# A new order and a new choice of engines for one fused attention, MLP and expert program

## The chip, the cores and the metric

The kernel runs on one core of one Trainium2 chip. The metric is the device time of one execution in microseconds, the median of several runs. The kernel before takes 794.45 us (median of 3 runs, 793.1 to 795.2). A difference under 0.3%, some 2.4 us, is about what a measurement of this kernel can't tell from no change.

## The reference, cut to what matters

Three layers follow each other: attention with two kinds of masks, an MLP whose gate is a cosine, and a layer with 8 experts that takes each token once, by a greedy assignment with a capacity.

```python
scores = scale * np.matmul(q, k.transpose(0, 1, 3, 2))     # 4 batches, 8 heads, 576 positions, 64
attn = softmax(where(mask, scores, -1e9))                  # heads 0-3: the last 32 positions; 4-7: every 32nd
x = (attn @ v) as [2304, 512]
h = x @ w_in;  g = h * np.cos(h);  y = g @ w_out           # 512 -> 2048 -> 512
logits = y @ w_gate                                        # 8 experts
for idx in np.argsort(-logits.flatten()):                  # a token to its best expert with room, 288 each
    ...
for e in range(8):
    out[mask] = np.maximum(y[mask] @ w1[e], 0.0) @ w2[e]   # 512 -> 1024 -> 512
```

Products are made in float16 with a high and a low part: each is three matrix products (high by high, high by low, low by high).

## The kernel before, in words

**Stages.** Attention of batch 0 and 1 in float32 and of batch 2 and 3 in float16 parts (`att_pair` L622, `att_half` L709). Layer 1 of the MLP in units of 128 columns of `w_in` (`l1_unit` L873): 24 products of 128 x 288 a unit, then on ACT and DVE the cosine and its two float16 parts, which lie in `ar_a`, `ar_b` and `ar_t`. Layer 2 in tiles of 128 tokens (`l2_tile` L986), 18 tiles, written to `y_dram`. The assignment (`route` L1021) is a long chain of small DVE instructions, and the matrix products of the last 13 tiles lie beside it on PE. The experts (`experts` L1213) end the program.

**The experts.** `expert_weights` (L1195) brings the weights of one expert in 8 loads of 512 KB from `w` into two staging buffers (`wst`, in `ar_l`). A load is made into float16 parts in two halves: for each half an ACT instruction writes the high part (an ACTIVATE of 128x512 that reads `ar_l`, into `ar_l` for experts of even number and into `ar_a` for those of odd number), then a DVE instruction writes the low part. A staging buffer is free for its next load when both of its DVE instructions are done. `layer1` (L1241) makes 8 groups of 12 products of 128 x 288 on PE; each group is taken out of PSUM by a relu on ACT (an ACTIVATE `ar_w<-psum`) and a DVE instruction for the low part. `layer2` (L1263) makes 8 groups for 4 outputs, taken out by an ACTIVATE `ar_b<-psum`. `gather` (L1219) fetches the tokens of the next expert and transposes them by DMA (3 DMA_TRANSPOSE of `ar_b`), and `store` (L1283) transposes the outputs by DMA (3 DMA_TRANSPOSE of `ar_w`), copies them and writes them out. All direct loads, stores and DMA transposes are issued by SP, in one order.

**What sets the order.** The function that describes the work doesn't issue it: every instruction, or group of matrix products, is a task that `Plan.add` (L179) records with its engine, a duration by a formula, and what it reads and writes. `Plan.order` (L217) is a list scheduler that runs when the kernel is built: it follows the engines in time, takes on each free engine the ready task with the longest path to the end, and so fixes each engine's order of instructions. On the chip each engine goes through its order as it stands. Three tables steer it: `BOOST` (L53) adds a number to the path of the tasks of one label, `CHOICE` (L97) puts an optional task on another engine (`'gl'`: the low part of the cosine on DVE or POOL, `'oh'` and `'og'`: copies of the store, `'cvo'`: the conversion of a block of `w_out`, `'exp'`: the way in which the exponential gets its bias), and `LAT` (L165) is the wait between two engines. Up to the first product with a block of `w_out`, gaps on PE that the scheduler foresees are filled with products that nobody reads (`p.filler`, L507).

Of the kernel before, what the change touches and what calls it, by code (L numbers as in the profile page):

```python
# [48 lines left out]
SWITCH = 1283.0  # L49
# [4 lines left out]
    ('att', 0, 0, 1): 579, ('att', 0, 0, 2): 6896, ('att', 0, 0, 3): 656, ('att', 0, 0, 4): 23690, ('att', 0, 1, 0): 1726,  # L54
    ('att', 0, 1, 1): 2601, ('att', 0, 1, 2): 5980, ('att', 0, 1, 3): -29, ('att', 0, 1, 4): 1804, ('att', 0, 2, 0): -529,
    ('att', 0, 2, 1): 5908, ('att', 0, 2, 2): 723, ('att', 0, 2, 3): 25775, ('att', 0, 2, 4): -70, ('att', 0, 3, 0): 1022,
    ('att', 0, 3, 1): 2929, ('att', 0, 3, 2): 209, ('att', 0, 3, 3): 20612, ('att', 0, 3, 4): 6402, ('att', 1, 0, 0): 1630,
    ('att', 1, 0, 1): 4760, ('att', 1, 0, 2): 4942, ('att', 1, 0, 3): 452, ('att', 1, 1, 0): 1309, ('att', 1, 1, 1): -15332,
    ('att', 1, 1, 3): -14442, ('att', 1, 1, 4): 7781, ('att', 1, 2, 0): -16993, ('att', 1, 2, 1): -7431, ('att', 1, 2, 2): -161,
    ('att', 1, 2, 3): -1353, ('att', 1, 2, 4): 964, ('att', 1, 3, 0): -28626, ('att', 1, 3, 1): 278, ('att', 1, 3, 2): 7133,  # L60
    ('att', 1, 3, 3): 1662, ('att', 1, 3, 4): -8348, ('att', 2, 0, 0): -6066, ('att', 2, 0, 1): -2444, ('att', 2, 0, 2): -7600,
    ('att', 2, 0, 3): 2071, ('att', 2, 1, 0): 596, ('att', 2, 1, 1): 2386, ('att', 2, 1, 2): -693, ('att', 2, 1, 3): -642,
    ('att', 2, 1, 4): -4, ('att', 2, 2, 0): -405, ('att', 2, 2, 1): 1129, ('att', 2, 2, 2): 2285, ('att', 2, 2, 3): 500,
    ('att', 2, 2, 4): 1102, ('att', 2, 3, 0): 12272, ('att', 2, 3, 1): 243, ('att', 2, 3, 2): 23127, ('att', 2, 3, 3): -4806,
    ('att', 2, 3, 4): 56132, ('att', 3, 0, 0): 3915, ('att', 3, 0, 1): 1009, ('att', 3, 0, 2): -6033, ('att', 3, 0, 3): 3149,
    ('att', 3, 0, 4): -31510, ('att', 3, 1, 1): -1244, ('att', 3, 1, 2): -1327, ('att', 3, 1, 3): 2204, ('att', 3, 1, 4): -3113,
    ('att', 3, 2, 0): 6530, ('att', 3, 2, 1): 3150, ('att', 3, 2, 3): 7677, ('att', 3, 2, 4): 21602, ('att', 3, 3, 0): 40114,
    ('att', 3, 3, 1): 25986, ('att', 3, 3, 2): 17764, ('att', 3, 3, 3): 815, ('att', 3, 3, 4): 28249, ('l1', 0, 0): 195,
# [26 lines left out]
}  # L95

CHOICE = {  # L97
# [1419 lines left out]
```

## Time and profile before

| | |
|---|---|
| median of 3 runs | 794.45 us (793.1 to 795.2) |
| the profiled execution | 796.68 us |
| its span, first to last instruction | 794.3 us |
| PE busy | 717.5 us (90%) |
| DVE, ACT, POOL busy | 527.4, 409.7, 275.7 us |
| mean granted TensorE clock | 0.974 |
| DMA | 104.14 MB, mean 131 GB/s |

The profiled execution is one run, 2.2 us above the median of the others; its span leaves out 2.4 us around the instructions. An engine's busy time is the time in which an instruction of its own runs; what an engine waited for is told in the list of waits, and windows give the busy time of each engine in a stretch of the span.

### The profile page before, as it was taken

How to read it: one execution, taken by the hardware profiler on the slowest of the kernel's cores; microseconds unless marked ns; L12 is line 12 of the kernel's file. 1: busy time of each engine (PE TensorE's matmuls, PEld its weight loads, DVE VectorE, ACT ScalarE, POOL GpSimd, SP SyncE). 2: the span in 40 equal slices, each digit the busy share in tenths (PEclk: the TensorE clock that was granted, in tenths of full speed). 3: DMA queues.
4: the chain of work that ended last, by engine and by line, in shares of the span. 5: the costliest groups of instructions: out<-in, count | busy, mean ns of one | idle time of the engine just before them, and what ended most of it. 6: DMA issues, size and time to landing. Idle time of an engine off the chain costs nothing.

```text
span 794.3 us, 18699 instructions
## 1 busy us (share of the span) xinstructions
PE 717.5 (90%) x7520; PEld 497.4 (63%) x7520; DVE 527.4 (66%) x1356; ACT 409.7 (52%) x907; POOL 275.7 (35%) x292
## 2 busy tenths in 40 slices
PE   7878888988998998999999999999898988789896
PEld 6666666764543676777654554335786766567686
DVE  4799999995767788756487777578346455644620
ACT  3556877875643689888440111024135554654532
POOL 2667476666531145335100000001521343231231
PEclk8999999999999999999899999999899999999998
DMA  8954254555767742000252000016588999989731
GB/s 241 286 167 130 72 146 114 146 130 121 165 136 194 162 96 54 20 1 1 67 162 78 28 28 14 15 43 195 139 171 209 256 246 220 241 232 238 167 71 41
DMA packets 114262, 104.14 MB, mean 131 GB/s; under 512 B 79872, under 2 KB 89856, under 8 KB 114176
## 3 DMA queue, kind: packets, MB, share of 16 engines
q1 hardware_dynamic: 111104, 93.52, 46.1%
q0 software_dynamic: 3072, 9.44, 3.8%
q8 instruction: 59, 0.97, 0.5%
q14 instruction: 27, 0.22, 0.1%
HBM read 74.36 MB, written 9.70 MB: 106 GB/s over the span
## 4 chain that ended last, share of the span: by engine, by line
PE 33%; DMA 26%; DVE 22%; ACT 12%; issue 4%; POOL 2%; SPq 1%; POOLq 0%; ACTq 0%; DVEq 0%
PE psum L358 32%; DMA ar_l<-w 14%; DVE ar_l L392 9%; DVE ar_t L392 7%; ACT ar_l L382 5%; DVE ar_a L392 3%; ACT ar_a L382 2%; ACT ar_t L382 2%; DMA ar_t<-w_in 2%; DVE ar_w L392 2%; DMA ar_b<-ar_b 1%; DMA ar_l<-ar_t 1%; DMA ar_b<-y_dram,idy 1%; DVE mxs L392 1%; DMA ar_t<-w_out 1%
## 5 line engine op out<-in xcount | busy, mean ns | idle before, releaser
L358 PEld LDWEIGHTS <-ar_l 128*128 128x128 f16 x2576 | 232.8, 99 | 99.0 <-issue 34.5
L358 PE MATMUL psum<-ar_l 128*128 128x288 f16 (+2 forms) x1578 | 205.9, 287 | 23.2 <-DVE ar_l L392 22.9
L358 PEld LDWEIGHTS <-ar_a 128*128 128x128 f16 (+1 forms) x1600 | 128.7, 99 | 94.9 <-issue 41.8
L358 PE MATMUL psum<-ar_w,ar_a 128*128 128x512 f16 (+3 forms) x1056 | 175.0, 310 | 5.6 <-DVE ar_w L392 2.3
L382 ACT ACTIVATE ar_l<-psum 128x288 int32<-128x288 f32 (+5 forms) x201 | 78.2, 412 | 92.5 <-PE psum L358 79.4
L392 DVE SCALAR_TENSOR_TENSOR ar_l<-ar_l,psum 128x288 f32<-128x288 int32 (+2 forms) x236 | 98.2, 441 | 36.1 <-ACT ar_l L382 34.8
L358 PEld LDWEIGHTS <-ar_t 128*128 128x128 f16 (+4 forms) x1980 | 74.6, 101 | 42.3 <-issue 19.0
L382 ACT ACTIVATE ar_a<-ar_l 128x512 f16<-128x512 f32 (+2 forms) x125 | 63.6, 537 | 54.6 <-DMA ar_l<-w 50.6
L392 DVE SCALAR_TENSOR_TENSOR ar_l<-ar_l 128x512 f16<-128x512 f32 (+3 forms) x94 | 52.2, 574 | 37.7 <-ACT ar_l L382 36.7
L382 ACT ACTIVATE ar_l<-ar_l,quarter 128x288 f32<-128x288 f32 x128 | 66.2, 530 | 12.6 <-DVE ar_l L392 12.0
L392 DVE SCALAR_TENSOR_TENSOR ar_t<-ar_t 128x512 uint32<-128x512 uint32 (+6 forms) x60 | 62.8, 1049 | 13.0 <-ACT ar_t L382 12.9
L392 DVE SCALAR_TENSOR_TENSOR ar_a<-ar_l,ar_a 128x512 f16<-128x512 f32 x64 | 43.5, 711 | 37.0 <-ACT ar_a L382 36.9
L437 POOL TENSOR_TENSOR ar_l<-ar_l 128x288 f32<-128x288 f32 (+1 forms) x41 | 28.0, 685 | 111.0 <-DVE ar_l L392 80.9
L382 ACT ACTIVATE ar_l<-ar_l 128x512 f16<-128x512 f32 x64 | 37.0, 621 | 55.4 <-DMA ar_l<-w 55.4
L358 PE MATMUL psum<-ar_w,ar_t 128*128 128x512 f16 (+2 forms) x288 | 63.8, 349 | 0.0
L382 ACT ACTIVATE ar_t<-ar_t 128x512 uint32<-128x512 uint32 (+12 forms) x63 | 46.2, 754 | 33.5 <-DVE ar_t L392 9.7
L358 PE MATMUL psum<-ar_w,ar_b 128*128 128x512 f16 (+1 forms) x240 | 62.6, 393 | 0.0
L358 PE MATMUL psum<-ar_b,ar_a 128*128 128x288 f16 (+3 forms) x504 | 55.2, 277 | 8.1 <-DVE ar_w L392 4.2
L358 PE MATMUL psum<-ar_b,ar_l 128*128 128x96 f16 (+1 forms) x576 | 51.2, 253 | 6.6 <-ACT ar_b L382 3.4
L1301 POOL DMA_INDIRECT out<-ar_b,idx x24 | 24.0, 999 | 84.4 <-DMA out<-ar_b,idx 18.6
L358 PE MATMUL psum<-ar_w,ar_l 128*128 128x288 f16 x384 | 47.9, 286 | 3.5 <-DVE ar_w L392 3.5
L437 POOL TENSOR_TENSOR ar_t<-ar_t 128x512 uint32<-128x512 uint32 (+7 forms) x25 | 40.5, 1623 | 20.5 <-ACT ar_t L382 19.9
(142 smaller groups left out, 881.2 us busy)
## 6 DMA issues: line engine op xcount, KB each, us to landing
ar_l<-w SPq DMA_DIRECT2D x64, 512.0 KB, 4.1
ar_t<-w_out SPq DMA_DIRECT2D x16, 512.0 KB, 3.5
ar_t<-w_in SPq DMA_DIRECT2D x12, 512.0 KB, 4.6
y_dram<-ar_l SPq DMA_DIRECT2D x13, 256.0 KB, 2.0
ar_t<-vl SPq DMA_DIRECT2D x6, 432.0 KB, 5.6
ar_t<-qs SPq DMA_DIRECT2D x4, 648.0 KB, 4.5
ar_t<-vs SPq DMA_DIRECT2D x6, 384.0 KB, 3.4
ar_t<-ql SPq DMA_DIRECT2D x4, 576.0 KB, 4.1
```

Source lines behind the costliest of these rows:

```text
L358: nc.tensor.matmul(o, l, x, start=start, stop=stop)
L382: p.add("act", ns, lambda: nc.scalar.activation(o, x, func, **kw), r, w, tab=tab)
L392: p.add("dve", 69.0 + 1.042 * n, lambda: getattr(nc.vector, name)(*args, **kw), r, w)
L437: p.add("pool", 145.0 + (rate or (1.667 if y.dtype == F32 else 1.885)) * size(o), lambda: nc.gpsimd.tensor_tensor(o, x, y, op=op), r, w)
L1301: p.add("pool", 546.0, lambda og=og, T=T: nc.gpsimd.indirect_dma_start(out[:, :], bass.IndirectOffsetOnAxis(ap=idx[:, T:T + 1], axis=0), o ...
```

## The change

`LAT` and the formulas for durations are new, and `Plan.order` is written anew. It now steps through time and follows all five engines side by side. A task on DVE and one on POOL that both carry the flag `ports` go at 0.62 and 0.77 of their rate while both run. A DMA takes SP 400 ns to issue (a transpose 152 ns for each 128 columns), and its data pass one after the other through one server with a first wait, a time by size (`work`), and at most 8 DMAs in flight. The tables `BOOST` and `CHOICE` were found anew with it. The instructions' arithmetic stays.

```diff
 BOOST = {
-    ('att', 0, 0, 1): 579, ('att', 0, 0, 2): 6896, ('att', 0, 0, 3): 656, ('att', 0, 0, 4): 23690, ('att', 0, 1, 0): 1726,
...
+    ('att', 0, 0, 0): -180, ('att', 0, 0, 1): -62086, ('att', 0, 0, 2): -8815, ('att', 0, 0, 3): -3820, ('att', 0, 0, 4): 19790,
...
 CHOICE = {
...
+    ('cvi', 0): 'pool', ('cvi', 2): 'pool', ('cvi', 9): 'pool2', ('cvi', 10): 'pool', ('cvi', 14): 'pool', ('cvo', 3): 'pool2',
...
-    LAT = {"pe": {"pe": 3.0, "act": 197.0, "dve": 196.0, "pool": 200.0, "sp": 1290.0},
-           "act": {"pe": 200.0, "act": 60.0, "dve": 142.0, "pool": 170.0, "sp": 1410.0},
...
-           "sp": {"pe": 740.0, "act": 908.0, "dve": 908.0, "pool": 908.0, "sp": 2100.0},
+    LAT = {"pe": {"pe": 3.0, "act": 197.0, "dve": 196.0, "pool": 200.0, "sp": 200.0},
+           "act": {"pe": 200.0, "act": 60.0, "dve": 142.0, "pool": 170.0, "sp": 140.0},
...
+           "sp": {"pe": 450.0, "act": 450.0, "dve": 450.0, "pool": 450.0, "sp": 300.0},
+    BESIDE = {"dve": 0.62, "pool": 0.77}
+    FIRST, FIRST_POOL, FLIGHT = 950.0, 1100.0, 8
...
-    def add(self, eng, ns, fn, r=(), w=(), tab=None, lat=None, busy=None):
+    def add(self, eng, ns, fn, r=(), w=(), tab=None, work=None, busy=None, ports=False, late=0.0):
...
     def order(self):
...
+        def rate(e):
+            i = cur[e]
+            if e == "pe":
+                look(int(now / self.WINDOW + 1e-9))
+                return 1.0 if warm[int(now / self.WINDOW + 1e-9)] else t[i][1] / self.busy[i][0]
+            if e in self.BESIDE and t[i][6]:
+                o = cur["pool" if e == "dve" else "dve"]
+                if o is not None and t[o][6]:
+                    return self.BESIDE[e]
+            return 1.0
...
+                if e == "sp":
+                    server = max(now + self.FIRST, server) + t[i][5]
+                    land[i] = server
+                    lands.append(server)
...
     def dma(o, x, nbytes, r, w):
-        p.add("sp", nbytes / 360.0, lambda: nc.sync.dma_start(o, x), r, w)
+        p.add("sp", 400.0, lambda: nc.sync.dma_start(o, x), r, w, work=nbytes / (390.0 if any(k[0] == "y" for k in w) else 240.0))
 
     def dma_t(o, x, r, w):
 
-        p.add("sp", 112.0 * x.shape[1] / 128, lambda: nc.sync.dma_start(o, x, transpose=True), r, w)
+        p.add("sp", 152.0 * x.shape[1] / 128, lambda: nc.sync.dma_start(o, x, transpose=True), r, w, work=160.0 * x.shape[1] / 128)
```

**What moves, on ACT, in layer 1 of expert 2.** `ar_w<-psum` is a relu of `layer1`, `ar_a<-ar_l` the high part of half a load of expert 3, `ar_l<-ar_l` of expert 4, and the COPY belongs to the store of expert 1. Before, from the first of these relus on:

```order
L382 ACTIVATE ar_w<-psum 128x288 x3
L382 ACTIVATE ar_a<-ar_l 128x512 x2
L382 ACTIVATE ar_w<-psum 128x288
L382 ACTIVATE ar_a<-ar_l 128x512 x2
L382 ACTIVATE ar_w<-psum 128x288
L385 COPY ar_b<-ar_w 96x512
L382 ACTIVATE ar_w<-psum 128x288
L385 COPY ar_b<-ar_w 96x512
L382 ACTIVATE ar_l<-ar_l 128x512
L382 ACTIVATE ar_w<-psum 128x288
L382 ACTIVATE ar_l<-ar_l 128x512
L382 ACTIVATE ar_w<-psum 128x288
```

And with the change, from the first relu of the same layer on:

```order
L417 ACTIVATE ar_w<-psum 128x288
L417 ACTIVATE ar_a<-ar_l 128x512 x2
L417 ACTIVATE ar_w<-psum 128x288 x3
L417 ACTIVATE ar_a<-ar_l 128x512 x2
L417 ACTIVATE ar_w<-psum 128x288
L420 COPY ar_b<-ar_w 96x512 x2
L417 ACTIVATE ar_w<-psum 128x288
L420 COPY ar_b<-ar_w 96x512
L417 ACTIVATE ar_w<-psum 128x288
L417 ACTIVATE ar_a<-ar_l 128x512 x2
L417 ACTIVATE ar_w<-psum 128x288
L420 COPY ar_b<-ar_w 96x512
```

Six halves of loads stand among the eight relus in both. Before they are the last two loads of expert 3 and the first of expert 4; now they are the fourth, fifth and sixth load of expert 3. Counted in loads, the conversions ahead of the first relu of layer 1 of the experts 1 to 7 were 22, 30, 38, 46, 53.5, 60 and 64, and are 21, 27, 33, 39, 45, 53 and 61 (8 loads belong to each expert, and layer 1 of expert e needs 8e + 4 of them).

**On ACT, layer 1 of expert 7.** Here `ar_a<-ar_l` is a half load of expert 7 itself. The rows before, from the second last load of the program on, through layer 2 of expert 6 (`ar_b<-psum`) and layer 1 of expert 7:

```order
L382 ACTIVATE ar_a<-ar_l 128x512 x2
L382 ACTIVATE ar_w<-psum 128x288
L382 ACTIVATE ar_a<-ar_l 128x512 x2
L382 ACTIVATE ar_w<-psum 128x288 x2
L382 ACTIVATE ar_b<-psum 128x288 x2
L385 COPY ar_w<-ar_b 128x3x96
L382 ACTIVATE ar_b<-psum 128x288 x2
L385 COPY ar_w<-ar_b 128x3x96 x2
L382 ACTIVATE ar_w<-psum 128x288 x6
L385 COPY ar_b<-ar_w 96x512
L382 ACTIVATE ar_w<-psum 128x288 x2
```

With the change, from the first relu of layer 1 of expert 7 on:

```order
L417 ACTIVATE ar_w<-psum 128x288 x2
L417 ACTIVATE ar_a<-ar_l 128x512 x2
L417 ACTIVATE ar_w<-psum 128x288 x2
L420 COPY ar_b<-ar_w 96x512 x2
L417 ACTIVATE ar_w<-psum 128x288
L420 COPY ar_b<-ar_w 96x512
L417 ACTIVATE ar_w<-psum 128x288
L417 ACTIVATE ar_a<-ar_l 128x512
L417 ACTIVATE ar_w<-psum 128x288
L417 ACTIVATE ar_a<-ar_l 128x512
L417 ACTIVATE ar_w<-psum 128x288
L417 ACTIVATE ar_a<-ar_l 128x512 x2
```

The last two loads were converted among the relus of expert 6, and the eight relus of expert 7 found all weights there. Now six halves, three loads, stand among the relus of expert 7, the last load behind all of them.

**On SP, the loads and transposes of the first experts.** `ar_l<-w` is a load, DMA_TRANSPOSE of `ar_w` the store of an expert, of `ar_b` the gather for the next. Before, from the third load of expert 2 on:

```order
L440 DMA ar_l<-w 128x1024 x2
L440 DMA ar_l<-w 128x2x512 x4
L444 DMA_TRANSPOSE ar_w<-ar_w 128x8x128 x3
L440 DMA ar_l<-w 128x1024 x2
L444 DMA_TRANSPOSE ar_b<-ar_b 128x8x96 x2
L440 DMA ar_l<-w 128x1024 x2
L444 DMA_TRANSPOSE ar_b<-ar_b 128x8x96
L440 DMA ar_l<-w 128x2x512 x3
L444 DMA_TRANSPOSE ar_w<-ar_w 128x8x128
L440 DMA ar_l<-w 128x2x512
L444 DMA_TRANSPOSE ar_w<-ar_w 128x8x128 x2
```

With the change, from the same load on:

```order
L478 DMA ar_l<-w 128x1024 x2
L478 DMA ar_l<-w 128x2x512 x2
L482 DMA_TRANSPOSE ar_w<-ar_w 128x8x128 x2
L478 DMA ar_l<-w 128x2x512
L482 DMA_TRANSPOSE ar_w<-ar_w 128x8x128
L478 DMA ar_l<-w 128x2x512
L478 DMA ar_l<-w 128x1024
L482 DMA_TRANSPOSE ar_b<-ar_b 128x8x96
L478 DMA ar_l<-w 128x1024
L482 DMA_TRANSPOSE ar_b<-ar_b 128x8x96 x2
L478 DMA ar_l<-w 128x1024 x2
```

The transposes of the first store stood behind six loads and stand behind four, and the third of them stands between two loads.

**Counts.** PE has 351 fillers for 185. Of the cosine's low parts of batch 0 and 1, seven go from DVE to POOL and five from POOL to DVE. The conversion of block 3 of `w_out` becomes `'pool2'`: two DVE instructions on 128x512 less, a DVE TENSOR_SCALAR, an ACT and two POOL instructions more. One pair of heads of batch 1 takes its exponentials with a bias (two DVE TENSOR_TENSOR from PSUM less, nine small ACTIVATE for two), so does one of batch 2. Batch 0 has one copy out of PSUM more on DVE and one less on ACT. ACT has 18 loads of function tables for 16. The softmax product of two pairs, and the low part of one, go from DVE to POOL in batches 2 and 3. The copies of the stores change places among ACT, DVE and POOL.

## Rows read from the trace of the kernel before

**Rows 1.** Windows: from:to, length, busy PE, PEld, DVE, ACT, POOL; clock; DMA share; GB/s.

```profile
100.00:120.00 20.00, 16.14 (x136) 12.45 (x135) 19.70 (x38) 15.61 (x40) 13.24 (x14) 1.00 0.53 139
...
200.00:220.00 20.00, 19.11 (x198) 11.65 (x196) 15.12 (x24) 15.37 (x23) 11.95 (x8) 1.00 0.75 149
...
460.00:480.00 20.00, 20.00 (x176) 10.29 (x175) 14.55 (x76) 1.92 (x3) 1.72 (x3) 1.00 0.07 27
...
640.00:660.00 20.00, 17.69 (x143) 13.71 (x141) 9.60 (x18) 9.70 (x22) 6.31 (x7) 1.00 0.90 234
```

**Rows 2.** What PE waited for, 590 to 770 us: total, times, longest.

```profile
PE psum L358 <- DVE ar_w L392: 13.3, 12, 2.2
PE psum L358 <- ACT ar_b L382: 7.1, 9, 1.5
```

**Rows 3.** What ACT waited for, 590 to 770 us.

```profile
ACT ar_l L382 <- DMA ar_l<-w: 36.8, 20, 7.5
ACT ar_a L382 <- DMA ar_l<-w: 35.9, 21, 4.1
```

**Rows 4.** Timeline of ACT, 628 to 640.5 us: start, length, instruction [idle before, releaser].

```profile
630.47 1.15 ACT L382 ACTIVATE ar_a<-ar_l 128x512 f16<-128x512 f32 x2 [2.50 <-DMA ar_l<-w]
...
634.33 1.15 ACT L382 ACTIVATE ar_a<-ar_l 128x512 f16<-128x512 f32 x2 [2.41 <-DMA ar_l<-w]
635.38 0.39 ACT L382 ACTIVATE ar_w<-psum 128x288 f16<-128x288 f32 x1
```

**Rows 5.** Timeline of PE, the same stretch.

```profile
633.35 1.63 PE L358 MATMUL psum<-ar_b,ar_l 128*128 128x288 f16 x12 [0.27 <-DVE ar_w L392]
637.21 3.47 PE L358 MATMUL psum<-ar_w,ar_l 128*128 128x288 f16 x27 [2.23 <-DVE ar_w L392]
```

**Rows 6.** Windows over the experts (columns as in rows 1).

```profile
601.90:768.50 166.60, 147.98 (x1166) 114.50 (x1165) 86.32 (x162) 87.94 (x190) 47.66 (x59) 0.99 0.86 215
...
602.00:663.80 61.80, 54.49 (x434) 42.16 (x432) 34.90 (x65) 34.78 (x76) 18.08 (x21) 1.00 0.98 242
```

**Rows 7.** Timelines of SP's DMA queue: start, length, issues.

```profile
585.95 15.41 SPq L440 DMA_DIRECT2D ar_l<-w  x6
...
706.29 1.94 SPq L440 DMA_DIRECT2D ar_l<-w  x2
...
715.82 8.24 SPq L440 DMA_DIRECT2D ar_l<-w  x4
...
744.41 1.04 SPq L440 DMA_DIRECT2D ar_l<-w  x2
```

**Rows 8.** Groups of DVE by form, 40 to 180 us: busy, mean ns | idle before.

```profile
L392 DVE SCALAR_TENSOR_TENSOR ar_t<-ar_t 128x512 uint32<-128x512 uint32 x37 | 35.5, 962 | 0.0
...
L392 DVE TENSOR_SCALAR ar_t<-ar_t 128x512 uint32<-128x512 uint32 x24 | 14.2, 591 | 0.4 <-DMA ar_t<-w_out 0.4
L392 DVE TENSOR_TENSOR ar_a<-ar_l,ar_a 128x288 f16<-128x288 f32 x13 | 8.0, 612 | 0.2
...
L392 DVE TENSOR_TENSOR ar_t<-psum,mxs 118x324 f32<-118x324 f32 x4 | 1.9, 483 | 0.0
```

**Rows 9.** Groups of POOL by form, 40 to 180 us.

```profile
L437 POOL TENSOR_TENSOR ar_a<-ar_l,ar_a 128x288 f16<-128x288 f32 x19 | 16.7, 885 | 13.4 <-ACT ar_a L382 13.4
...
L437 POOL TENSOR_TENSOR ar_t<-ar_t 128x512 uint32<-128x512 uint32 x10 | 13.6, 1356 | 6.2 <-ACT ar_t L382 6.2
```

**Rows 10.** Waits of PE, 90 to 193 us, then 193 to 385 us.

```profile
PE psum L358 <- DVE ar_l L392: 12.3, 10, 2.8
...
PE psum L358 <- DVE ar_l L392: 5.7, 5, 2.2
```

**Rows 11.** Timeline of PE, 50 to 58 us: one run of fillers and the product behind it.

```profile
52.86 3.23 PE L507 MATMUL psum<-quarter 128*128 128x128 f16 x52
56.55 0.32 PE L358 MATMUL psum<-mask,ident 128*128 128x384 bf16 x1 [0.46 <-ACT ar_t L608]
```

**Rows 12.** Groups of ACT: loads of function tables.

```profile
L382 ACT ACT_TABLE_LOAD x14 | 18.0, 1283 | 0.3
```

More of the change, by code (lines that the diff above doesn't have):

```diff
@@ L203, in add @@
         deps.discard(i)
-        self.tasks.append((eng, ns, fn, sorted(deps), tab, lat))
+        self.tasks.append((eng, ns, fn, sorted(deps), tab, work, ports, late))
         return i
@@ L215, in reuse, with wait, ways @@
         return i
-    def order(self):
+    def wait(self, i, s):
+        if self.tasks[s][0] is None:
+            return 0.0
+        return self.LAT["sp" if self.tasks[i][5] else self.tasks[i][0]][self.tasks[s][0]]
+    def ways(self):
         t = self.tasks
@@ L220, in order @@
         succ = [[] for _ in t]
-        left = [len(x[3]) for x in t]
         for i, x in enumerate(t):
@@ L240, in order @@
             path[i] = min(v for (m, _), v in top.items() if m == name) - L2_DELAY - 20.0 * k
+        return succ, path
+    def order(self):
+        t = self.tasks
+        succ, path = self.ways()
         for i, v in self.boost.items():
             path[i] += v
-        ready = [1700.0 if x[0] == "sp" else 500.0 for x in t]
-        avail = {}
-        free = {}
-        table = None
-        done = []
-        end = 0.0
+        left = [len(x[3]) for x in t]
+        ready = [700.0 if x[0] == "sp" else 500.0 for x in t]
+        avail = {e: [] for e in self.ENGINES}
+        now, server, table, recent, filling = 0.0, 0.0, None, 1.0, self.filler is not None
+        done, lands, land = [], [], {}
+        cur, rest, free = dict.fromkeys(self.ENGINES), {}, dict.fromkeys(self.ENGINES, 0.0)
         active, warm = [0.0], [False]
-        filling = [self.filler is not None]
-        recent = 1.0
         def look(win):
@@ L284, in push, with finish @@
             else:
-                avail.setdefault(t[i][0], []).append(i)
-        for i in range(n):
+                avail[t[i][0]].append(i)
+        def finish(i, at):
+            for s in succ[i]:
+                ready[s] = max(ready[s], at + self.wait(i, s))
+                left[s] -= 1
+                if left[s] == 0:
+                    push(s)
+        def rate(e):
[8 more added lines that the diff above has]
+            return 1.0
@@ new lines, in order @@
+        while True:
+            for e in self.ENGINES:
+                if cur[e] is not None or e == "sp" and len(lands) >= self.FLIGHT and lands[-self.FLIGHT] > now:
+                    continue
+                best = None
+                faded = recent * math.exp((free["pe"] - now) / 2500.0) if e == "pe" else 0.0
+                for i in avail[e]:
+                    if ready[i] <= now:
+                        v = path[i]
+                        if t[i][4] and table and t[i][4] != table:
+                            v -= SWITCH_PENALTY
+                        if e == "pe" and faded < 0.6 and self.busy[i][1] < 0.4 * t[i][1]:
+                            v -= LOW_PENALTY
+                        if best is None or v > best[0] or v == best[0] and i < best[1]:
+                            best = v, i
+                if best is None:
+                    continue
+                i = best[1]
+                avail[e].remove(i)
+                cur[e], rest[e] = i, t[i][1]
+                if e == "pe":
+                    fade = math.exp(-t[i][1] / 2500.0)
+                    recent = faded * fade + self.busy[i][1] / t[i][1] * (1.0 - fade)
+                    f = max(free["pe"], 700.0)
+                    while filling and f + 250.0 < now:
+                        win = int(f / self.WINDOW)
+                        look(win)
+                        done.append((f, -1))
+                        step = 55.3 if warm[win] else 106.7
+                        active[win] += step - 2.0
+                        f += step
+                    if i == self.fill_to:
+                        filling = False
+                if t[i][4]:
+                    if t[i][4] != table:
+                        rest[e] += SWITCH
+                    table = t[i][4]
+                if e == "sp":
+                    server = max(now + self.FIRST, server) + t[i][5]
+                    land[i] = server
+                    lands.append(server)
+                done.append((now, i))
+            at = 1e18
+            for e in self.ENGINES:
+                if cur[e] is not None:
+                    at = min(at, now + rest[e] / rate(e))
+                    if e == "pe":
+                        at = min(at, (int(now / self.WINDOW + 1e-9) + 1) * self.WINDOW)
+                else:
+                    for i in avail[e]:
+                        r = ready[i]
+                        if e == "sp" and len(lands) >= self.FLIGHT:
+                            r = max(r, lands[-self.FLIGHT])
+                        at = min(at, r)
+            if at > 1e17:
+                break
+            step = [(e, (at - now) * rate(e)) for e in self.ENGINES if cur[e] is not None]
+            for e, d in step:
+                rest[e] -= d
+                if e == "pe":
+                    i = cur[e]
+                    win = int(now / self.WINDOW + 1e-9)
+                    active[win] += self.busy[i][1] * (1.0 if warm[win] else 2.0) * d / t[i][1]
+            now = at
+            for e, _ in step:
+                if rest[e] <= 1e-6:
+                    i, cur[e] = cur[e], None
+                    free[e] = now
+                    if e == "pool" and t[i][5]:
+                        land[i] = max(now + self.FIRST_POOL, server) + t[i][5] + t[i][7]
+                        server = max(now, server) + t[i][5]
+                    finish(i, land.get(i, now))
@@ L330, in order @@
         assert sum(i >= 0 for _, i in done) == sum(x[0] is not None for x in t)
+        self.end = now
         return [t[i][2] if i >= 0 else self.filler for _, i in sorted(done)]
```

150 lines of the change are left out of this document (46 added, 104 removed), and 136 rows, old and new, of tables (BOOST, CHOICE).

## The prediction

> **What bounds the kernel now.** I read the windows of 20 us first, since the share of busy time over the whole span mixes stages that have different limits [rows 1]. From 100 to 120 us DVE is busy for 19.70 of 20 us and PE for 16.14: layer 1 of the MLP goes at the pace of DVE. From 460 to 480 us PE is busy all the time: the assignment's chain on DVE and the products of layer 2 lie side by side, and PE sets the pace. From 640 to 660 us, among the experts, PE is busy for 17.69 us, DVE and ACT for under half, and the DMA engines for 0.90 of the time.
>
> So I asked next what PE waits for among the experts. Between 590 and 770 us it waits 20.4 us, 13.3 for the DVE instruction that ends a group of layer 1 and 7.1 for the ACT instruction that ends one of layer 2 [rows 2]. Neither engine is short of time there. ACT itself waits 72.7 us for loads of `w` [rows 3]. The timeline shows how that reaches PE. ACT idles 2.41 us until the load for a conversion lands at 634.33, and only behind that conversion, at 635.38, comes the relu of a group that was ready before [rows 4]. PE, which needs the bank and the result, starts 2.23 us late, at 637.21 [rows 5]. A relu pays for a load that it doesn't need, because it stands behind it.
>
> How fast do the loads go? From layer 1 of expert 1 to layer 1 of expert 7, 601.90 to 768.50 us, PE goes through six experts in 166.6 us, 27.8 us each, and is busy for 148.0, 24.7 us each [rows 6]. On SP 44 loads lie between the issue at 585.95 and that at 744.41, so 3.60 us for one [rows 7]; eight, an expert's need, take 28.8 us. **The loads set the pace of the experts**, and the order before makes PE keep to it: it puts 6.5 to 8 loads of conversions between the first relus of one expert and the next, up to expert 6. PE thus ends with weights to spare: the last two loads are issued at 744.41, 50 us before the span's end.
>
> **The change, experts.** The new order keeps the loads and their number, but puts only 6 loads between the first relus of the experts 1 to 5, and 8 between those of 5 to 7 (21, 27, 33, 39, 45, 53, 61 against 22, 30, 38, 46, 53.5, 60, 64). The stock of weights is used up instead of kept. For four periods the loads need 6 x 3.60 = 21.6 us, less than PE's 24.7, so PE sets the pace: 4 x 24.7 = 98.8 us. For the last two, 16 loads bind. Their price I bound by two rows of SP. The six issues from 585.95 on end after 15.41 us: five steps of about 3.0 us [rows 7]. The slowest pair, with three transposes behind it, goes from 706.29 to 715.82: 4.76 us for one. I take 3.45, a little under the mean of 3.60, for part of the transposes now stand singly among the loads, while those of a store still hold up the loads behind them: 16 x 3.45 = 55.2 us. PE's waits will not all go; relus still stand behind conversions, six halves among eight relus in the two places shown. I leave a fifth of the 20.4 us, 4 us. Sum: 98.8 + 55.2 + 4 = 158 us against 166.6, **9 us less**. The ends: 148.0 us where the loads take 3.1 us or less and no wait is left (18.6 less), and 98.8 + 16 x 4.76 = 175 us (8.4 more).
>
> Behind the first relu of expert 7 three loads are still to come, 10.4 us. Seven more groups of layer 1, of 12 products, take 84 x 127 ns = 10.7 us (148.0 us over 1166 products, [rows 6]) and cover them; so the tail costs nothing, or 1 to 2 us if a load is late.
>
> **The change, layer 1 of the MLP.** Here DVE binds, so I count its work. Block 3 of `w_out`: two instructions of 962 ns less, one of 591 more, 1.3 us less [rows 8]. The exponentials of one pair: two of 483 ns less, 1.0 us. The low parts of the cosine: net two of 612 ns less, 1.2 us. One copy from PSUM more, by its nearest row some 0.5 us. That is 3.0 us less. POOL gets 2 x 0.885 + 2 x 1.356 = 4.5 us more [rows 9]. DVE groups are slower beside POOL in this stretch (a price between nothing and the whole 4.5 us); I take 2 us, as less than half of DVE's time is in the groups with two operands in SBUF. Left: 1 us less. The order itself: PE waits 12.3 us for DVE from 90 to 193 us and 5.7 us from there to 385 us [rows 10]. A planner that knows when DVE is slow could take some away, but an engine busy for 19.70 of 20 us has little to give: I take 2 us. Together **3 us less**, between 18 less (all those waits) and 1.5 more (the 4.5 us in full against 3.0).
>
> **The change, the rest.** The 166 new fillers cost 62 ns each by a run of 52 in 3.23 us, 10.3 us in all. Behind that run the next product still waits 0.46 us for ACT [rows 11]: fillers lie in gaps that PE has anyway, in the first 90 us. I take nothing, with 10.3 us as the end should the gaps be shorter than the scheduler believes; the cover would be gone where the inputs arrive earlier. Two more table loads of 1.28 us [rows 12] lie on ACT, busy for 15.61 of 20 us. The moves in batches 2 and 3 lie beside PE at 19.11 of 20, those in the assignment beside PE at 20.00 [rows 1]: nothing.
>
> **Sum.** The profiled execution took 796.68 us. Less 9 and 3 that is 784.7. It stands 2.2 us above the median of the runs, 794.45, so for a median I forecast **782.5 us**, within 775 to 791 by this case alone.
>
> **The rivals.** *More is won*: the loads don't bind at all and PE goes through six experts in 148.0 us, with 6 us from the waits for DVE: 794.45 - 18.6 - 6 = 770 us. For it speaks the fastest stretch of 3.0 us a load; against it that the DMA engines are already busy for 0.98 of the time from 602 to 663.8 us while they move 242 GB/s [rows 6]. The Trainium skill's page "SBUF — State Buffer", section "A bandwidth-pool intuition that's wrong", gives some 358 GB/s from HBM to a core; by that the eight loads of an expert (4.19 MB) would need an estimated 11.7 us, far less than PE, and this rival would hold. No row here comes near that rate, so I follow the rows.
>
> *The waits change places*: every load that PE no longer lags behind, a relu waits for elsewhere. For it speaks that the pattern of halves among relus is the same in both orders; against it the 6 loads in a period, 21.6 us, which PE can't catch up with. Then nothing is won in the experts and 0 to 1 us before them: 794 us.
>
> *The stock is missed*, slower: from expert 5 on PE stands at the start of each layer until a load lands. The order allows it, since the first relu of expert 7 has only 61 loads ahead where 60 are needed, and 64 were there before. At the slowest pair's 4.76 us a load the experts take 175 us, and the time is 794.45 + 8.4 - 2 = 801 us. It decides from (166.6 - 98.8) / 16 = 4.24 us a load on. The mean of 3.60 speaks against it; that the store's transposes now come two loads earlier, and must wait for data of a layer that has just ended, speaks for it.
>
> **The numbers.** The forecast has 0.62, more won 0.12, the waits that change places 0.13, the missed stock 0.13. About 0.3%, 2.4 us, is what a measurement can tell from no change. So faster 0.74, same 0.13, slower 0.13. The range from 771 to 796 us takes in the forecast, the case of no change and half of the case that wins more, and leaves out the missed stock: 0.81 is within.
>
> **What would show it.** Right: six experts on PE in about 158 us; PE's waits there near 10 us, and the longest of them at the start of layer 1 of the experts 6 and 7; loads some 4.1 us apart up to expert 5 and 3.5 after; the last load issued some 30 us before the span's end instead of 50; layer 1 of the MLP done some 3 us earlier. Wrong: relus that still wait 2 us behind conversions in the experts 1 to 4 (the waits change places), loads over 4.2 us apart after expert 5 (the missed stock), or a first 90 us that grow by several us with PE busy on fillers.

## The result, and the profile after

The change takes 781.91 us (median of 4 runs, 780.32 to 784.46), the kernel before beside it 793.97 us: a ratio of 0.985, 95% interval 0.982 to 0.988, so 12 us less (9.5 to 14.3). The profiled execution of the change took 780.32 us, its span is 778.5. It lies 1.6 us under the median of its kind and that of before 2.2 to 2.7 over its own, so the two spans differ by 15.8 us, more than the medians do.

The page of the change, its first lines:

```profile
span 778.5 us, 19060 instructions
...
PE 721.5 (93%) x7686; PEld 502.3 (65%) x7686; DVE 527.7 (68%) x1348; ACT 419.6 (54%) x928; POOL 281.8 (36%) x297
```

PE is busy 4 us longer than before, in a span 15.8 us shorter: 11 us more with fillers, 7 us less with all other products. The windows that answer to [rows 1], and one near the end of the experts (columns as there):

```profile
100.00:120.00 20.00, 15.87 (x125) 11.88 (x123) 18.89 (x38) 15.62 (x38) 15.91 (x15) 1.00 0.43 121
...
200.00:220.00 20.00, 19.61 (x145) 10.34 (x143) 11.54 (x19) 8.79 (x13) 12.27 (x8) 1.00 0.59 150
...
460.00:480.00 20.00, 20.00 (x178) 10.31 (x175) 14.46 (x76) 2.51 (x4) 1.72 (x3) 1.00 0.07 27
640.00:660.00 20.00, 19.85 (x163) 15.71 (x161) 11.54 (x18) 11.89 (x25) 8.54 (x13) 1.00 0.98 230
700.00:720.00 20.00, 17.24 (x125) 12.42 (x124) 9.37 (x18) 10.26 (x20) 3.03 (x4) 0.91 0.85 209
```

Layer 1 of the MLP still goes at DVE's pace. Among the experts, where PE was busy for 17.69 of 20 us, it is now busy for 19.85; only from 700 us on gaps come back.

**Where the time went.** PE's first product with gathered tokens starts at 563.7 us in before and at 563.8 in the change, the last of layer 2 of expert 7 ends at 786.2 and 768.7. The whole gain lies between. Windows over the six experts and over the stretch that answers to [rows 6]:

```profile
602.00:663.80 61.80, 61.65 (x504) 49.06 (x502) 31.18 (x53) 35.61 (x75) 27.18 (x37) 1.00 0.99 244
591.50:741.30 149.80, 144.26 (x1153) 112.97 (x1152) 84.97 (x153) 86.99 (x184) 49.32 (x62) 0.99 0.91 231
```

From the first product of expert 1 to that of expert 7 it is 149.8 us; in before it was 166.6 (594.6 to 761.2; the stretch of [rows 6] begins and ends four groups later, with the same length). Expert 0 ahead of that stretch takes 27.7 us instead of 30.9, expert 7 behind it 27.4 instead of 25.0, and what follows the last product 9.8 instead of 8.1. PE's timeline shows the new pace, 96 products of layer 1 and 96 of layer 2 in turn, without a stop from 605.42 to 699.82 but for 0.15 us:

```profile
601.02 4.57 PE L393 MATMUL psum<-ar_b,ar_a 128*128 128x288 f16 x36 [1.38 <-DVE ar_w L429]
605.42 11.92 PE L393 MATMUL psum<-ar_w,ar_a 128*128 128x288 f16 x96
617.18 11.92 PE L393 MATMUL psum<-ar_b,ar_l 128*128 128x288 f16 x96
628.95 11.92 PE L393 MATMUL psum<-ar_w,ar_l 128*128 128x288 f16 x96
640.71 11.92 PE L393 MATMUL psum<-ar_b,ar_a 128*128 128x288 f16 x96
```

What PE, then ACT, waited for between 590 and 770 us, against [rows 2, 3]:

```profile
PE psum L393 <- DVE ar_w L429: 3.5, 6, 1.4
PE psum L393 <- ACT ar_l L417: 2.1, 2, 1.3
...
ACT ar_a L417 <- DMA ar_l<-w: 23.5, 17, 2.7
ACT ar_l L417 <- DMA ar_l<-w: 22.7, 14, 9.2
```

With three small ones PE waits 7.0 us instead of 20.4. ACT still waits 46.2 us for loads, of 72.7, and relus and outputs still stand behind such waits. Here it is an output in layer 2 of expert 2, behind a wait of 2.38 us:

```profile
637.48 1.15 ACT L417 ACTIVATE ar_a<-ar_l 128x512 f16<-128x512 f32 x2 [2.38 <-DMA ar_l<-w]
638.54 0.39 ACT L417 ACTIVATE ar_b<-psum 128x288 f32<-128x288 f32 x1
```

PE runs on through it, as its row from 628.95 on shows; in [rows 4, 5] a wait of 2.41 us cost it 2.23. What makes that difference was not followed.

The loads themselves are no faster. SP's queue, against [rows 7]:

```profile
584.25 10.03 SPq L478 DMA_DIRECT2D ar_l<-w  x4
...
696.03 4.62 SPq L478 DMA_DIRECT2D ar_l<-w  x2
...
720.44 23.93 SPq L478 DMA_DIRECT2D ar_l<-w  x9
...
749.90 1.06 SPq L478 DMA_DIRECT2D ar_l<-w  x2
```

44 loads lie between the issues at 584.25 and 749.90, 3.76 us each; in before it was 3.60. The last load goes out 28 us before the span's end, not 50.

**Before the experts.** I split the time up to them into four windows; the first four rows are the change's, the last four those of before:

```profile
0.00:90.00 90.00, 79.61 (x1196) 64.77 (x1197) 74.29 (x153) 55.41 (x129) 44.95 (x52) 0.98 0.63 186
90.00:265.00 175.00, 159.92 (x1635) 102.34 (x1634) 134.90 (x254) 109.41 (x252) 99.39 (x88) 0.99 0.56 138
265.00:400.00 135.00, 122.95 (x1507) 95.60 (x1507) 90.24 (x209) 110.21 (x249) 52.25 (x52) 0.97 0.22 58
400.00:563.80 163.80, 161.48 (x1372) 80.03 (x1370) 123.35 (x544) 32.32 (x55) 16.24 (x25) 0.99 0.23 73
```

```profile
0.00:90.00 90.00, 75.29 (x1065) 58.65 (x1066) 73.35 (x155) 50.99 (x123) 47.75 (x53) 0.92 0.65 190
90.00:265.00 175.00, 154.71 (x1527) 99.92 (x1526) 140.73 (x262) 112.67 (x253) 90.13 (x81) 0.98 0.57 138
265.00:400.00 135.00, 127.89 (x1600) 98.26 (x1597) 90.14 (x211) 105.92 (x241) 54.16 (x55) 0.97 0.24 60
400.00:563.70 163.70, 157.60 (x1356) 77.81 (x1353) 119.88 (x536) 32.10 (x55) 15.79 (x24) 1.00 0.21 69
```

The same windows of the fillers' line alone give 26.92 us (x351) and 15.89 us (x185) in the first 90 us. So the change is busy there with real products for 52.7 us and before for 59.4. Not all of these 6.7 us is work that the change has still to do, since before makes its products at a mean clock of 0.92 and the change at 0.98. By number it is 845 products against 880, some 2.3 us at the 62 to 68 ns that one takes on average in these two windows. From 90 to 265 us the change does 5.2 us more, from 265 to 400 us 4.9 us less, in the assignment 3.9 us more. At the experts the two are level, with 5359 and 5363 real products by these rows. So what the change has won by 265 us is lost again by 400.

### The profile page after: what moved, and what is told of

Its sections match the earlier page's. It is cut to its first block, busy times and chain, and to the rows that moved or that the text cites. A ratio compares the mean times of both kernels' runs of the same rounds, so it can differ in the third digit from the quotient of the medians.

```text
span 778.5 us, 19060 instructions
## 1 busy us (share of the span) xinstructions
PE 721.5 (93%) x7686; PEld 502.3 (65%) x7686; DVE 527.7 (68%) x1348; ACT 419.6 (54%) x928; POOL 281.8 (36%) x297
## 4 chain that ended last, share of the span: by engine, by line
PE 36%; DVE 20%; DMA 17%; ACT 12%; POOL 5%; issue 5%; SPq 3%; POOLq 0%; DVEq 0%; ACTq 0%
PE psum L393 36%; DMA ar_l<-w 8%; DVE ar_l L429 7%; DVE ar_t L429 7%; ACT ar_l L417 5%; DVE ar_a L429 3%; ACT ar_t L417 3%; ACT ar_a L417 2%; SPq L482 2%; POOL ar_t L474 2%; DMA ar_t<-vl 1%; DMA ar_t<-w_in 1%; DVE mxs L429 1%; POOL ar_l L474 1%; DVE ar_w L429 1%
## 5 line engine op out<-in xcount | busy, mean ns | idle before, releaser
L393 PEld LDWEIGHTS <-ar_l 128*128 128x128 f16 x2576 | 230.1, 98 | 94.0 <-issue 30.2
L393 PEld LDWEIGHTS <-ar_t 128*128 128x128 f16 (+3 forms) x1980 | 76.2, 102 | 40.1 <-issue 20.7
L429 DVE SCALAR_TENSOR_TENSOR ar_l<-ar_l 128x512 f16<-128x512 f32 (+3 forms) x94 | 55.3, 610 | 31.3 <-ACT ar_l L417 30.1
L429 DVE SCALAR_TENSOR_TENSOR ar_t<-ar_t 128x512 uint32<-128x512 uint32 (+6 forms) x58 | 56.5, 978 | 14.8 <-ACT ar_t L417 14.4
L393 PE MATMUL psum<-ar_w,ar_b 128*128 128x512 f16 (+1 forms) x240 | 66.3, 399 | 0.0
L393 PE MATMUL psum<-ar_b,ar_a 128*128 128x288 f16 (+3 forms) x504 | 53.0, 272 | 2.4 <-DVE ar_w L429 1.6
L474 POOL TENSOR_TENSOR ar_t<-ar_t 128x512 uint32<-128x512 uint32 (+7 forms) x28 | 46.2, 1653 | 19.6 <-ACT ar_t L417 16.3
L393 PEld LDWEIGHTS <-ar_b 128*128 128x128 f16 (+2 forms) x392 | 28.6, 100 | 26.3 <-issue 8.1
```

The costliest lines, as they stand in the source:

```text
L393: nc.tensor.matmul(o, l, x, start=start, stop=stop)
L429: p.add("dve", 69.0 + 1.042 * n, lambda: getattr(nc.vector, name)(*args, **kw), r, w, ports=both)
L474: p.add("pool", 145.0 + (rate or (1.667 if y.dtype == F32 else 1.885)) * size(o), lambda: nc.gpsimd.tensor_tensor(o, x, y, op=op), r, w, p ...
```

## The experiments

Most of these kernels issue their tasks in a written-out order. Where nothing else is said, the edit is that of the loop that issues them, with another list:

```diff
-    for emit in p.order():
-        emit()
+    for i in ORDER:
+        (p.tasks[i][2] if i >= 0 else p.filler)()
```

Periods are the times from the first product of one expert's layer 1 to that of the next, for experts 1 to 7, read from PE's timeline.

**1 and 2. Each half of the change alone.** The list of the first holds the change's order up to the experts and before's from there, with the copies' engines (`'og'`, `'oh'`, `'yt'` of `CHOICE`) of before; that of the second the reverse.

> The change's order (and its choice of engines) up to the first product of the experts, at 563.7 us, and the order and copies of before from there on. Theory A, that the whole gain comes from the experts since both orders reach the first of them at 563.7 and 563.8 us: 794 us, as before. By the split of the prediction (9 us in the experts, 3 us in layer 1 of the MLP): 791 us. Theory B, that the experts run faster because of what the new order leaves them (more converted weights, a higher clock): 784 to 788 us.

> The other half: the order of before up to the first product of the experts, and the change's order and copies from there on. Theory A: 781 us, within 1.5 us of the change, six experts in about 150 us. By the split of the prediction: 785 us. Theory B: 787 to 792 us, with the periods of the experts nearer 27.7 us than 23.6.

Measured: 795.91 us for the first, beside 797.71 for before, ratio 0.9994 (0.9965 to 1.0022); 780.51 us for the second, ratio 0.9825 (0.9766 to 0.9884). The periods of the second are 25.0, 23.5, 23.5, 24.3, 23.5 and 30.4 us, those of the change 25.6, 23.5, 23.8, 23.5, 23.5 and 29.7. Theory A holds: the experts' order is the gain, and all that is new ahead of them is worth -0.5 us (-2.8 to +1.8).

**3. Only the conversions and loads moved, in before.**

> The order of before and its choice of engines; only the conversions of the experts' weights on ACT and DVE and the loads on SP are moved behind the relu, output or transpose (counted from the first) behind which the change has them: 21, 27, 33, 39, 45, 52 and 61 loads converted ahead of the first relus of experts 1 to 7. Theory A1, that the number of loads between one expert and the next is what sets the pace: 780 to 784 us, the experts 2 to 6 in 23.5 to 24.5 us each. Theory A2, that the order of the groups on PE and the engines of the store's copies do it: 790 to 794 us, periods of 27 to 28 us.

Measured: 794.45 us, ratio 0.9967 (0.9937 to 0.9997). The time is that of theory A2, the periods are those of neither: 27.5, 27.5, 23.5, 24.2, 27.4 and 35.5 us. The stock is used up as in the change, and while it lasts PE hardly waits:

```profile
640.00:700.00 60.00, 59.49 (x487) 47.37 (x486) 30.84 (x58) 32.60 (x72) 20.14 (x27) 1.00 0.87 217
700.00:760.00 60.00, 46.67 (x355) 34.74 (x353) 26.55 (x51) 28.44 (x60) 10.99 (x15) 0.97 0.72 185
```

But the loads are slower: from the first of expert 2 to the last of all 4.57 us each, where before has 4.11 and the change 4.19 (a longer stretch than that of the 44 loads above, so other means). A likely cause shows on SP: the loads now stand behind transposes whose copies come where they came before, and from 575 to 770 us SP waits 12.2 us for DVE ahead of such transposes, which isn't among its longer waits in the change. 47 loads at 0.38 us are 18 us, and eat what the stock gives.

**6. The reverse: the change with the conversions and loads put back.**

> The change, with only the conversions and loads of the experts' weights put back behind the relu, output or transpose (counted from the first) behind which before has them: 22, 29, 38, 46, 53.5, 60 and 64 loads ahead of the first relus of experts 1 to 7. The third experiment slowed the loads themselves (4.6 us each where the change has 4.2), so it decided little; here the loads are early and can't be held up by relus. Theory A1, that eight loads between one expert and the next tie PE to the loads: PE loses what it won, within 6 us of the kernel before, periods of 27 to 29 us with loads still 4.1 to 4.2 us each. Theory A2, that the order of the groups on PE and the copies' engines win it: 12 us or more under the kernel before, periods under 25 us.

Measured: 820.93 us, ratio 1.0323 (1.0272 to 1.0374), slower than both, and neither theory. Periods of 37.6, 35.7, 30.0, 29.2, 29.4 and 31.1 us; the loads take 4.61 us here, against what I expected; why was not followed. PE's longest waits from 575 to 790 us:

```profile
PE psum L457 <- DVE ar_w L493: 32.0, 18, 5.4
PE psum L457 <- ACT ar_b L481: 8.4, 7, 3.0
```

Runs 3 and 6 have loads of the same pace, 4.57 and 4.61 us, and differ in where PE's groups stand among the conversions. That is what tells, read from the timelines of DVE (end of the last conversion of the first four loads of expert 7) and PE (first product of its layer 1):

| | loads, us each | weights converted | first product |
|---|---|---|---|
| before | 4.11 | 737.5 | 761.2 |
| run 6 | 4.61 | 757.2 | 784.5 |
| the change | 4.19 | 744.0 | 741.3 |
| run 3 | 4.57 | 759.4 | 755.8 |

In the two upper kernels the weights of layer 1 lie ready 24 to 36 us before PE uses them, in each of the experts 2 to 7; in the two lower ones that stock shrinks from 23 to 25 us at expert 2 to 7 to 9 us at expert 4, and from expert 5 on PE starts on the first halves while the last are converted. Run 3 reaches expert 7 at 755.8 us, run 6 at 784.5: 28.7 us at the same pace of loads. The two also differ in the copies' engines, so the stock's price alone is not to be had from them. At the same stock, run 3, whose loads take 0.38 us longer, comes 14.5 us behind the change. Both parts are needed: the stock must be spent, and the copies and transposes must be moved with it so that the loads keep their pace.

**8. Before, with smaller loads.**

```diff
-                dma(st.rearrange("p (k f) -> p k f", f=wd),
-                    a[name][e, 128 * k:128 * (k + kk), :].rearrange("(k p) f -> p k f", p=128), 524288, [], [("wst", si)])
+                dma(st.rearrange("p (k f) -> p k f", f=wd)[:64],
+                    a[name][e, 128 * k:128 * (k + kk), :].rearrange("(k p) f -> p k f", p=128)[:64], 524288, [], [("wst", si)])
```

> The kernel before, order and all, with each load of the experts' weights cut to 64 of its 128 partitions, half the bytes (the other half of a staging buffer is zero, so the experts compute with half their weights). If loads set the pace of the experts in before: 15 to 20 us less than before, periods near 24 us, and ACT's waits for loads mostly gone. If the order of the groups and of the copies holds PE up: under 5 us less, PE still waiting for relus that stand behind copies.

Measured: 778.24 us (one run), 19 us less than before. Periods of 25 to 27 us, not the 24 I expected; the loads take 3.79 us each, and PE followed them: the weights of expert 7 are ready at 719.6 (17.9 us earlier than in before), its first product at 742.8 (18.4 earlier), and the 23 us between stay. So in before the loads set the pace, and the order of groups and copies did not keep PE from following them. That this order would hold up nothing at still faster loads isn't shown. ACT's waits for loads, 58.8 us, are not mostly gone as I had expected, since a load of half the bytes is hardly shorter (last section).

**4. Four staging buffers, the order found anew.**

```diff
-                si, st = rot("wst", wst)
+                si, st = rot("wst", wst)
+                sk = ("wst" if si < 2 else "wsx", si)
...
+    p.reuse(["gx"], ["wsx"])
+    wst += [ar_t.t[:, 1024 * i:1024 * i + 1024] for i in range(STAGES - 2)]
```

> The change with two more staging buffers for the loads of the experts 1 to 7, in a part of the memory that is free by then, and the order found anew by the same scheduler. Theory C, that with two buffers a load waits for its conversions and so the loads fall behind PE in the last period (29.7 us where the others take 23.6): 776 us, the last period 24 to 25 us. Theory D, that the DMA engines, busy for 0.9 to 0.99 of the time in the experts, can move no more: 781 to 783 us, no change. A third case, that the order comes out differently and loses what the tuned tables won: 785 us or more.

Measured: 808.93 us, ratio 1.0157 (1.0107 to 1.0207): the third case, though PE's last period is 23.5 us, even less than theory C had. The windows, and the row of SP that tells why:

```profile
564.00:764.00 200.00, 197.47 (x2016) 162.57 (x2013) 105.31 (x191) 110.77 (x242) 57.64 (x69) 1.00 0.86 211
764.00:810.00 46.00, 0.07 (x1) 0.00 (x0) 2.86 (x7) 6.73 (x12) 12.90 (x15) 0.54 0.28 70
```

```profile
738.70 36.62 SPq L484 DMA_TRANSPOSE ar_w<-ar_w  x7
```

PE waits 0.2 us from 575 to 790 us and is done at 764, five us before the change. But stores were put off behind loads: seven of their transposes are left when the last load is out, and eleven scatters to `out` follow one another from 766.90 to 804.55 us. The loads take 3.48 us each here, counted as in the third experiment. Whether the buffers made them faster or the stores that no longer stood among them, this run can't tell; the next keeps the stores in their places.

**5. The second kernel with four buffers, every engine's order kept.**

```diff
+    more += wst + [ar_t.t[:, 1024 * i:1024 * i + 1024] for i in range(2)]
...
-                si, st = rot("wst", wst)
+                si, st = rot("wst", wst if e < 2 else more)
+                sk = ("wst" if si < 2 else "wsx", si)
```

> The kernel of the second experiment (order of before up to the experts, the change's from there on) with two more staging buffers for the loads of experts 2 to 7, every engine's order kept: on SP the loads keep their places among the transposes, so the stores can't be put off as they were in the fourth experiment. Theory C, two buffers bind the last period: 3 to 6 us less than the second experiment, which was 17 us under the kernel before, so 20 to 23 us under it; last period 25 to 27 us where it was 30.4. Theory D, the DMA engines bind: 16 to 18 us under the kernel before, last period still 29 us or more.

Measured: 773.43 us, ratio 0.971 (0.9675 to 0.9745), 23.8 us under the 797.24 of before: better than both kernels. The sum is a little better than theory C had, but the last period is the one of theory D, still 29.1 us, 1.3 less. The rest of the gain is in the first one (23.9 for 25.0), in the fourth (23.5 for 24.3) and behind the last (25.0 us from the first product of expert 7 to the end of its layer 2, 27.3 in the second kernel). So two more buffers are worth something, but they do not by themselves shorten the last period: with the same four buffers it was 23.5 us in run 4, where the stores were put off.

**9 and 10. Loads two places earlier on SP; and the same with the change's first part.**

> The fifth experiment (order of before up to the experts, four staging buffers), with every load from the fifth of expert 2 on put two loads earlier in SP's order, ahead of the transposes that stood between. In the fifth experiment the last period was still 29.1 us, and SP waited 24.4 us for copies on ACT while no load could go out. If that block on SP holds the last period up: 768 to 771 us, last period 24 to 26 us, about 27 us under the kernel before. If the DMA engines or ACT's order of conversions hold it up: 772 to 775 us, as the fifth experiment. If stores now wait behind loads that wait for a buffer: 776 us or more, with a longer tail.

> The same four buffers and earlier loads, but the change's order from the first instruction on. If the part up to the experts is worth the same in both orders, as both reach the experts at 563.7 and 563.8 us: within 2 us of the kernel beside it, which has the order of before up to there. If the change's first part costs something that one profile hid: 2 to 5 us more.

Measured: 774.1 us, ratio 0.972 (0.9688 to 0.9753), and 773.92 us, ratio 0.9723 (0.9693 to 0.9754). The block on SP was not it: the last period of run 9 is 29.0 us, 5.5 above PE's pace. PE waits 4.5 us in it, 1.8 for the conversions of expert 6's first weights and 2.7 for relus. Its timeline and that of ACT show the latter, in layer 1 of expert 6:

```profile
719.51 1.63 PE L423 MATMUL psum<-ar_b,ar_l 128*128 128x288 f16 x12 [0.50 <-DVE ar_w L457]
723.34 4.57 PE L423 MATMUL psum<-ar_b,ar_l 128*128 128x288 f16 x36 [2.19 <-DVE ar_w L457]
```

```profile
721.77 0.76 ACT L450 COPY ar_b<-ar_w 96x512 uint16<-96x512 uint16 x1 [3.19 <-DMA ar_w<-ar_w]
722.40 0.69 ACT L447 ACTIVATE ar_w<-psum 128x288 f16<-128x288 f32 x2
```

It is the pattern of [rows 4, 5] with another DMA: a copy of the store waits 3.19 us for its transpose, and the relus behind it pay. Whether these copies on another engine would give the 2.7 us back wasn't tried. Run 10 shows once more that the part ahead of the experts is worth the same in both orders.

**7, 11 and 12. Half of the fillers, none, and the change again.** The edit is that of run 11; run 7 leaves out every second filler only.

```diff
     for emit in p.order():
-        emit()
+        if emit is not p.filler:
+            emit()
```

> The change with every second one of its 351 fillers left out, 176 left, about as many as before has. As the prediction has it, that fillers lie in gaps: the time of the change, 10 to 15 us under the kernel before, and the first 90 us hold the same work. If the fillers are in the way of products that are ready: up to 5 us less than the change. If they keep the granted clock up and that matters: 2 to 6 us more, with a lower clock in the first 90 us.

> The change with none of its 351 fillers. With half of them left out it was about 4 us slower and its granted clock in the first 90 us 0.86 to 0.91 where the change has 0.97 to 1.00. If the fillers pay by the clock: 5 to 10 us more than the change run beside it, clock under 0.85 in the first 90 us. If that difference was chance, and fillers cost and bring nothing: within 1.5 us of the change.

> The change as it is, on the same chip as the three others, so that they can be set against it: 0.985 of the kernel before, between 0.982 and 0.988.

Measured: 788.99 us with half of them, ratio 0.9898 (0.9851 to 0.9944); 789.6 us with none, ratio 0.9924 (0.9897 to 0.9951); 782.9 us for the change beside it, ratio 0.9843 (0.9796 to 0.9889). So all 351 fillers together are worth 6.7 us, at the lower end of the first case of run 11. Run 7 ran beside other runs of before, so the ratios are to be compared: the half that it keeps gains some 2 us and the half that it leaves out some 4, with intervals that overlap. The windows of the first 90 us without fillers, then those of the change beside it:

```profile
0.00:45.00 45.00, 35.25 (x449) 25.03 (x450) 26.28 (x62) 19.68 (x54) 16.73 (x24) 0.81 0.84 241
45.00:90.00 45.00, 31.71 (x339) 23.19 (x336) 39.51 (x81) 30.76 (x65) 24.87 (x25) 0.73 0.41 121
```

```profile
0.00:45.00 45.00, 42.29 (x659) 34.54 (x660) 31.29 (x69) 23.82 (x64) 18.91 (x27) 1.00 0.88 255
45.00:90.00 45.00, 37.64 (x540) 30.22 (x539) 42.92 (x85) 31.71 (x66) 26.14 (x26) 0.96 0.37 117
```

Where PE idles between the products of the first stage, the granted clock falls from its upper level, 2.4 GHz, to the lower, 1.2, for part of the time, and the mean of the second window is 0.73; layer 1 of expert 0 starts at 576.1 us instead of 568.0. By these rows 788 real products are done in the 90 us without fillers and 848 with them, so the fillers are not in the way.

## Why the prediction was right, and where its steps were not

The time, 781.91 us against 782.5, and the sign came out as said. That it came out so near is in part luck: by runs 1 and 2 the term for the experts was some 5 us too small and the one for layer 1 of the MLP some 2.5 us too large.

**What bounds the experts: right.** The loads set the pace of before (run 8), and the new order wins by spending the stock that before kept (runs 1, 2, 3 and 6). The windows show it, the last load out 28 us before the end was forecast as 30, and the loads' pace, 3.76 us each over the whole, did not improve. From 584.25 to 696.03 us 29 loads went out, 3.85 us each, where I had some 4.1 up to expert 5. From the last load of expert 5 on, at 696.03, 15 loads went out up to 749.90, 3.59 us each for the 3.45 I took, well under the 4.24 from which the stock would have been missed. PE's waits, 7.0 us, were forecast as near 10. Their place is half right: four of 0.3 to 1.3 us stand at the start of layer 1 of expert 6, but hardly one at that of expert 7, and the longest, 1.4 us, in layer 1 of expert 1.

**The experts' term: mis-sized.** I had 9 us less, 158 us for six experts; it was 149.8, 16.8 less, and behind it 2.4 us more. Expert 0, which the sum left out, gave 3.2 us besides. Three numbers of the sum were too high.
- *4 x 24.7 us at PE's pace*: the four periods took 25.6 + 23.5 + 23.8 + 23.5 = 96.4. PE's busy time in before was not its pace. One of its six periods, from 705.80 us on, had 25.71 us of it at a mean clock of 0.94. And at a clock of 1.00, for the same 192 to 194 products before shows 24.27 us in a period with waits and the change 23.50 in one without, as these two windows tell (before, then the change):

```profile
594.60:622.30 27.70, 24.27 (x192) 18.69 (x192) 16.28 (x32) 16.21 (x36) 6.00 (x8) 1.00 0.92 227
```

```profile
617.20:640.70 23.50, 23.50 (x194) 18.75 (x192) 11.68 (x21) 14.41 (x31) 10.80 (x14) 1.00 0.99 244
```

- *16 loads x 3.45 = 55.2 us for the last two periods*: 23.5 + 29.7 = 53.2. The stock lasted one period longer. What the last one takes above PE's pace is not loads alone: PE waits 3.6 us in it, and after the first waits the clock falls, so that the same products keep it busy for 26.00 us instead of 23.50:

```profile
711.60:741.30 29.70, 26.00 (x195) 19.15 (x192) 16.96 (x33) 16.21 (x34) 5.73 (x6) 0.94 0.77 213
```

- *4 us of waits on top*: those that remained lie inside the periods above.

**The tail: off by a little.** I had nothing, or 1 to 2 us if a load is late. From the first product of expert 7 to the end of its layer 2 it took 25.0 us in before and 27.4 in the change.

**Layer 1 of the MLP: wrong.** I counted 3 us less there, 1 from DVE's work and 2 from PE's waits, and took the rest as nothing. DVE's work fell, by 5.8 us from 90 to 265 us, and POOL's rose by 9.3; PE did 5.2 us more of products there. But PE's waits for DVE moved instead of going away. From 90 to 193 us and from there to 385 us they were 12.3 and 5.7 us [rows 10], and with the change:

```profile
PE psum L393 <- DVE ar_l L429: 9.2, 11, 2.0
...
PE psum L393 <- DVE ar_l L429: 9.1, 9, 2.3
```

What is won by 265 us is gone by 400, and the part up to the experts as a whole is worth nothing that can be measured (run 1). A first 90 us that grow by several us with PE busy on fillers stood among the signs of being wrong; the change is some 2.3 us behind there, and fillers are not the cause.

**Fillers at nothing: wrong in sign.** They are not in the way; they hold up the clock. All 351 are worth 6.7 us (run 11), and the half that run 7 leaves out, about as many as are new, some 4. I priced only their time on PE, not what the gaps would cost without them. The products that the change is behind at 90 us are so not lost to fillers but to the order; which of the moves there did it was not tried.

**The rivals.** *More won* gave 148.0 us for the six experts, nearer than my own number, but for a reason that does not hold: the loads do bind, in the last period. Its page, the Trainium skill's "SBUF — State Buffer", section "A bandwidth-pool intuition that's wrong", has 358 GB/s; over the six experts the core moved 231 GB/s with the DMA engines busy for 0.91 of the time. *The waits change places* and *the missed stock* did not come about as a whole; run 9 shows the first of them in one period. The sign that I gave for that case, relus that wait 2 us behind conversions in the experts 1 to 4, was a poor one: an output of expert 2 still stands behind such a wait, and PE does not lose by it.

Terms of the runs together: -14.0 us for the experts (run 2's ratio of its 797.71, -9.3 to -18.7) and -0.5 for the rest, against 12 us measured (9.5 to 14.3). The intervals meet; a finer split is not to be had from them.

## What to carry to other kernels

Put the time at which an input is ready beside the time at which it is used, for every round of a loop: a distance that stays the same until the end is a stock that was paid for and never spent, and an order that spends it can win that distance once. When conversions are moved for that, look at the copies and transposes that share a queue with the loads: where they were not moved along (runs 3 and 6), the loads slowed from 4.1 or 4.2 us to 4.6 and took the gain back. Two more buffers won where every queue kept its order (run 5), and lost where the order found anew put the stores behind the loads (run 4).

## What the runs showed of the hardware that I had not expected

A load of the experts' weights over 64 partitions, 256 KB, lands in 3.7 us (median of the page), one over 128 partitions, 512 KB, in 4.1: half the bytes save a tenth of the time. The Trainium skill's page "SBUF — State Buffer", section "Door 1: The DMA port swizzle", says that partitions 0 to 63 reach only half of the memory's ports, so that such a transfer goes at about half the rate; the trace agrees, with 71 GB/s for one such load (262 KB in 3.7 us) and 128 for a whole one, from issue to landing and with other transfers beside them. Run 8's loads and its stores of as many bytes from all 128 partitions to `y_dram`, then the loads of before:

```profile
ar_l<-w SPq DMA_DIRECT2D x64, 256.0 KB, 3.7
y_dram<-ar_l SPq DMA_DIRECT2D x13, 256.0 KB, 2.0
```

```profile
ar_l<-w SPq DMA_DIRECT2D x64, 512.0 KB, 4.1
```

The stores go the other way, so they are a hint and no proof; how much of a load's time doesn't depend on its size, no run separates.

In these profiles PE's busy time grows with its waits: 0.77 us more for the same products in a period that is interrupted, at a clock of 1.00 in both, so the busy time of a stretch with waits is not the pace that the stretch would have without them.

Beside POOL, DVE waits rather than goes slower, which the flag `ports` has as a rate. A SCALAR_TENSOR_TENSOR of 128x512 on `ar_t` takes 0.68 us alone in before. The one at 99.67 us starts while a POOL TENSOR_TENSOR runs, from 99.17 to 100.41, and takes 1.28 us, to 0.55 us after that one's end. So it is in all 22 cases of before that start beside such an instruction: they end 0.545 to 0.555 us after it, though it had between 0.30 and 1.10 us left. What the scheduler would find with a wait in place of the rate was not tried.
